# Gated linear attention and a two-layer block on one core: the fourth unit's output transposed by DMA instead of TensorE, in an order written out as tables

## The chip, the cores and the metric

The kernel runs on one core of a Trainium2 chip. The metric is device time in microseconds (us); lower is better. A "unit" below is a piece of 256 tokens of one batch element; the units are numbered 0 to 11, so the fourth unit is unit 3.

## What is computed

The reference is a recurrent linear attention with a decay per channel, followed by a dense block of two layers with a squared ReLU. The shapes are B = 4, H = 8, S = 768, D = 48, and the dense block has 3072 tokens, width 384 and hidden width 2048; everything comes in and goes out as float32.

```
state = zeros(B, H, D, D)
for t in range(S):
    state = alpha[:, :, t, :, None] * state + k[:, :, t] (outer) v[:, :, t]
    y[:, :, t] = q[:, :, t] @ state
x = y with the heads side by side, one row of 384 for each token
out = (relu(x @ w_in) ** 2) @ w_out
```

## The kernel before

**Units.** The sequence is cut into three stretches of 256 tokens, which gives 12 units (`G`). For each unit g the four inputs alpha, k, q, v are loaded (`lda`, `ldk`, `ldq`, `ldv`, line 568, 384 KB each) into one of four raw buffers. ScalarE takes logarithms and exponentials of the decays (`lm`, `ln`, `ei`, `ea`, `ec`, `es`), TensorE sums them along the tokens (`m1i`), VectorE multiplies them into the queries and keys (`bk`, `ekm`, `eqm0`, `eqm1`), and `vc` casts v to bf16. From unit 3 on, queries and keys are transposed by two DMAs (`tr0`, `tr1`, line 762). TensorE then forms the scores (`p0`, line 940, into the PSUM tiles psX and psZ), VectorE masks them (`mk0`, `mk1`, line 951), TensorE forms the attention output in psX and the next unit's state in psZ (`y`, lines 832, 843, 811), VectorE updates the state (`sa`, `sc`, `sd`), and ScalarE copies the output to the bf16 tile xbf (`xe`, line 971).

**Transpose of the output.** The dense block needs the output with channels on the partitions, in one of four buffers xt. In units 0 to 3 TensorE does this with six transposing products into psX (`xt`, line 986) and VectorE or ScalarE copies the result to xt (`xv`, line 998 or 1000; for unit 3 it is ScalarE, line 1000). In the units of `DMA_X`, 4 to 11, one DMA that SyncE issues transposes xbf into xt (`xt`, line 992, 196,608 bytes), with the same bytes in another order, and the first layer reads xt with a stride that undoes that.

**Dense block.** The first layer of a unit is eight operations `s1_g_u` of six matmuls each (line 1042), which alternate between two PSUM banks of psWH. Each is followed by a ReLU (`re`, line 1050 on ScalarE or 1052 on VectorE), and then a square (`sq`, lines 1060 and 1064). The second layer is, for each half j of the unit's tokens, four operations `s2_g_j_0` to `s2_g_j_3` of four matmuls each (line 1089). They all accumulate into one PSUM bank, psO, which ScalarE or VectorE copies out (`oe_g_j`, line 1097 or 1099) before the other half may start. SyncE stores the unit (`out`, line 1109).

**Order.** The body of the kernel adds operations with the data that they read and write, a cost and a priority. `schedule` runs a model of the engines and of the queues, gives each operation an engine and a place in that engine's order, and a dictionary `SHIFT` moves single priorities. `fill` puts products on a tile of zeros (line 1143) into TensorE's idle times before the first dense products. `place` then decides which operation waits for which semaphore. Each engine executes its own list strictly in order, and so does SyncE, which issues nearly all DMAs: an operation that waits holds all that are behind it on that engine. Some starts are tied by hand: `lda` of a unit waits for the landing of the unit's before `ldq`, and `ldq` waits for the landing of the DMA `tr0` of the unit before.

**The stretch around the change.** Before the change the engines' lists are these (the text under the prediction uses the names):

```
TensorE  y3 m1i5 s2_2_0_0 s2_2_0_1 xt3 s2_2_0_2 s2_2_0_3 p0_4 s1_3_0 s2_2_1_0 .. s2_2_1_3 s1_3_1 s1_3_2 y4
         s1_3_4 s1_3_3 m1i6 s1_3_6 ..
ScalarE  re2_6 xe3 ei5 ea5 ec5 xv3 es5 oe2_0 re3_0 oe2_1 lm6 re3_1 ln6 xe4 re3_4 re3_3 ei6 ..
VectorE  sa4 sq2_6 sc4 bk5 sd4 lb5 ekm5 eqm1_5 eqm0_5 mk0_4 mk1_4 re3_2 ..
SyncE    lda5 ldk5 tr0_4 tr1_4 ldq5 ldv5 out1_1 lda6 ldk6 tr0_5 tr1_5 out2_1 xt4 ldq6 ldv6 lda7 ..
```

Of the kernel before, what the change touches and what calls it, by code (L numbers as in the profile page):

```python
# [2 lines left out]

# [3 lines left out]
ALU = mybir.AluOpType  # L7
# [7 lines left out]
class Op:  # L15


    __slots__ = ("alts", "eng", "fn", "cost", "prio", "deps", "idx", "lag", "sem", "start", "end", "pos", "name",
                 "users", "ndeps", "mode", "ready", "land")

    def __init__(self, alts, prio, name):
        self.alts, self.prio, self.name = alts, prio, name
        self.eng = self.fn = self.cost = None
        self.deps = {}
        self.lag = 0
        self.sem = None
        self.users = []
        self.pos = None
        self.mode = ("F", "F")
        self.ready = 0.0  # L30
        self.start = self.end = self.land = None


class Program:

    HOP = 35
    PE_LATENCY = 170
    DMA_FIRST = {"sp": 1300, "act": 1300, "pool": 2000}  # L40
    PACKET = (("win", 172), ("wout", 490), ("ld", 22), ("tr", 18), ("xt", 18), ("out", 125))
    SBUF_ONLY = ("pr", "bk", "aq", "ekm", "eqm", "sq", "sb", "sd")
    BIAS = {"pool": 300}
    DMA_LAST = {"sp": 800, "act": 800, "pool": 1900}
    SWITCH = 95
    HALVED = {"qks": 3, "kqt": 3, "raw": 3, "ek": 3, "eq": 3, "acm": 2, "laf": 2}
    AFFINITY = 2500

    SHIFT = {
        "aq2": -248, "aq3": -1491, "bk2": 5224, "bk3": -2010, "bk5": 1601, "bk6": -3855, "ea0_0": 13157,  # L50
        "ea1": -1949, "ea1_0": 12558, "ea2": 2000, "ea3": -1980, "ea4": -1414, "ea5": -2487, "ea6": 81,
        "ec0_0": 20747, "ec1": -746, "ec1_0": 11544, "ec2": 2000, "ec3": -2160, "ec4": -1533, "ec5": 2471,
        "ei0_0": 10906, "ei1": -1289, "ei1_0": 11939, "ei2": 2000, "ei3": 8259, "ei4": -2378, "ei5": 98, "ei6": -386,
        "ekm0_0": 11970, "ekm1": -1066, "ekm1_0": 10619, "ekm2": 5424, "ekm3": -1183, "ekm4": 175, "ekm5": 937,
        "ekm6": 1068, "eqm0_0": 12087, "eqm0_3": -1862, "eqm0_4": 3228, "eqm0_5": 3013, "eqm0_6": -440, "eqm1": 2398,
        "eqm1_0": 12786, "eqm1_3": 1310, "eqm1_4": 270, "eqm1_5": -275, "eqm1_6": -211, "eqm2": 2240, "es2": 2000,
        "es3": -2890, "es5": -2113, "es6": -1558, "et00_0": -6783, "et01_0": 2965, "et0_1": 18, "et0_2": 4740,
        "et10_0": 1180, "et11_0": 849, "et1_1": -8121, "et1_2": 9290, "kv0": 1952, "kv1": -5798, "kv2": -10315,
        "lb4": -1797, "lb5": 195, "lb6": 67, "lm4": -1578, "lm5": -1529, "lm6": -1532, "ln0_0": 10550, "ln1": -409,
        "ln1_0": 17073, "ln2": 2000, "ln3": -2160, "ln4": 564, "ln5": 4370, "ln6": -283, "m10_0": 4838, "m11": -338,  # L60
        "m11_0": 9538, "m1i2": 2121, "m1i3": -533, "m1i5": 400, "m1i6": -1147, "m1s2": 2468, "m1s3": 3167,
        "mk0_0": -1001, "mk0_1": 9322, "mk0_2": 5670, "mk0_3": -10630, "mk0_4": 4794, "mk0_5": -4832, "mk1_0": -830,
        "mk1_1": 1380, "mk1_2": 4510, "mk1_3": -10630, "mk1_4": 7108, "mk1_5": -124, "oe0_0": -3484, "oe0_1": -14385,
        "oe1_0": -724, "oe1_1": 2594, "oe2_0": -260, "oe2_1": -627, "oe3_0": 11805, "oe3_1": 30, "oe4_0": -7260,
        "oe4_1": -7260, "oe5_0": 5260, "oe5_1": 5260, "out0_1": -8010, "out1_1": 6560, "out2_1": 2593, "out3_1": 30,
        "out4_1": -7260, "out5_1": 5260, "p0_0": -830, "p0_1": -2249, "p0_2": 4532, "p0_3": -11271, "p0_4": 2163,
        "p0_5": -6910, "p1_0": -830, "pr2": 376, "pr3": 563, "pr4": -2031, "pr5": 4470, "pr6": -3765, "pr7": -5581,
        "re0_0": -253, "re0_1": -2327, "re0_2": -1810, "re0_3": -2805, "re0_4": 7066, "re0_5": -3141, "re0_6": 1463,
        "re0_7": -2710, "re1_0": -2540, "re1_1": -1766, "re1_2": -2620, "re1_3": -2792, "re1_4": 4740, "re1_5": 99,
        "re1_6": -833, "re1_7": 2948, "re2_0": -151, "re2_1": -240, "re2_2": 24, "re2_3": -68, "re2_4": -519,  # L70
        "re2_5": -240, "re2_6": 5363, "re2_7": 3246, "re3_0": -3327, "re3_1": -1860, "re3_2": -1860, "re3_3": -2293,
        "re3_4": -1860, "re3_5": -5935, "re3_6": -6334, "re3_7": -1379, "re4_0": -5850, "re4_1": -2100,
        "re4_2": -6410, "re4_3": -2118, "re4_4": -5850, "re4_5": -5850, "re4_6": -5850, "re4_7": -5850,
        "re5_0": 2020, "re5_1": 2020, "re5_2": 2020, "re5_3": 2020, "re5_4": 2020, "re5_5": 2020, "re5_6": 2020,
        "re5_7": 2020, "s1_0_0": -2767, "s1_0_1": -1766, "s1_0_2": -1810, "s1_0_3": -1898, "s1_0_4": 202,
        "s1_0_5": -2691, "s1_0_6": -5306, "s1_0_7": 405, "s1_1_0": -2620, "s1_1_1": -5074, "s1_1_2": -364,
        "s1_1_3": 596, "s1_1_5": -6169, "s1_1_6": -383, "s1_1_7": -1034, "s1_2_0": -739, "s1_2_1": -687,
        "s1_2_2": -5198, "s1_2_3": -900, "s1_2_4": -1700, "s1_2_5": -240, "s1_2_6": -45, "s1_2_7": -688,
        "s1_3_0": -1860, "s1_3_1": -2146, "s1_3_2": -1582, "s1_3_3": -1860, "s1_3_4": -3211, "s1_3_5": -435,
        "s1_3_6": -1113, "s1_3_7": -1860, "s1_4_0": -10307, "s1_4_1": -5990, "s1_4_2": -5519, "s1_4_3": -6913,  # L80
        "s1_4_4": 2151, "s1_4_5": -6468, "s1_4_6": -5850, "s1_4_7": -5850, "s1_5_0": 2020, "s1_5_1": 2020,
        "s1_5_2": 2020, "s1_5_3": 2020, "s1_5_4": 2020, "s1_5_5": 2020, "s1_5_6": 2020, "s1_5_7": 2020,
        "s2_0_0_0": -7231, "s2_0_0_1": -6402, "s2_0_0_2": -9571, "s2_0_0_3": -4462, "s2_0_1_0": -7570,
        "s2_0_1_1": -6433, "s2_0_1_2": -7346, "s2_0_1_3": -13759, "s2_1_0_0": -1010, "s2_1_0_1": -1010,
        "s2_1_0_2": 6229, "s2_1_0_3": 4046, "s2_1_1_0": -1010, "s2_1_1_1": -4318, "s2_1_1_2": 7177, "s2_1_1_3": 9016,
        "s2_2_0_0": 4117, "s2_2_0_1": -1305, "s2_2_0_2": -260, "s2_2_0_3": -56, "s2_2_1_0": -6696, "s2_2_1_1": -5458,
        "s2_2_1_2": -259, "s2_2_1_3": -817, "s2_3_0_0": 690, "s2_3_0_1": 30, "s2_3_0_2": 3360, "s2_3_0_3": 3274,
        "s2_3_1_0": 30, "s2_3_1_1": 30, "s2_3_1_2": 30, "s2_3_1_3": 30, "s2_4_0_0": -7260, "s2_4_0_1": -7260,
        "s2_4_0_2": -7260, "s2_4_0_3": -7260, "s2_4_1_0": -7260, "s2_4_1_1": -7260, "s2_4_1_2": -7260,
        "s2_4_1_3": -7260, "s2_5_0_0": 5260, "s2_5_0_1": 5260, "s2_5_0_2": 5260, "s2_5_0_3": 5260, "s2_5_1_0": 5260,  # L90
        "s2_5_1_1": 5260, "s2_5_1_2": 5260, "s2_5_1_3": 5260, "sa0": 752, "sa1": -2890, "sa2": -10750, "sa3": 3302,
        "sa4": 2124, "sa5": -3013, "sc0": 873, "sc1": 490, "sc2": -9676, "sc3": 1435, "sc4": 2632, "sc5": -2325,
        "sd0": -4084, "sd1": 5380, "sd2": -10750, "sd3": 5505, "sd4": -5377, "sd5": -6091, "sq0_1": -2853,
        "sq0_3": -1810, "sq0_5": -3567, "sq0_6": -2710, "sq0_7": -7881, "sq1_1": 4005, "sq1_3": -2620, "sq1_5": 2964,
        "sq1_6": 101, "sq1_7": 3337, "sq2_1": 589, "sq2_3": -240, "sq2_5": -2358, "sq2_6": -240, "sq2_7": -2552,
        "sq3_1": -1736, "sq3_3": -1860, "sq3_5": -2116, "sq3_6": -1860, "sq3_7": 1961, "sq4_1": -2012,
        "sq4_3": -7277, "sq4_5": -5850, "sq4_6": -5850, "sq4_7": -5850, "sq5_1": 2020, "sq5_3": 2020, "sq5_5": 2020,
        "sq5_6": 2020, "sq5_7": 2020, "tr00_0": 1401, "tr01_0": 1210, "tr0_1": 1600, "tr0_2": 9290, "tr0_3": 329,
        "tr0_4": 730, "tr0_5": -1980, "tr0_6": -5474, "tr10_0": 505, "tr11_0": 3673, "tr1_1": 3514, "tr1_2": 14909,
        "tr1_3": 410, "tr1_4": 7738, "tr1_5": -1980, "vc0": 26092, "vc1": 2583, "vc2": 5594, "vc3": -2160,  # L100
        "vc4": 1938, "vc5": 859, "vc6": -1098, "xe0": 2520, "xe1": -5132, "xe2": 1303, "xe3": 9345, "xe4": 4442,
        "xe5": -2372, "xt0": -210, "xt1": -5759, "xt2": 697, "xt3": 5663, "xt4": 139, "xt5": 3570, "xv0": -3144,
        "xv1": -5170, "xv2": -2990, "xv3": 6300, "y0": -3305, "y1": -7643, "y2": -2990, "y3": 6489, "y4": 4090,
        "y5": -543,
    }

# [1068 lines left out]
```

## Time and profile before

| | |
|---|---|
| time, median of 3 runs | 174.98 us (174.0 to 175.28) |
| span of the profiled execution | 174.5 us |
| TensorE matmuls busy | 169.1 us, 97% of the span |
| VectorE, ScalarE, GpSimd busy | 121.3, 117.6, 18.8 us |
| share of the 16 DMA engines | 71.4% by SyncE's queue, 12.1% by GpSimd's |
| moved by DMA | 33.36 MB |

The profile states no time of its own for the profiled execution but its span, which lies from the first to the last instruction. The span is half a microsecond under the median of the runs and inside their spread. TensorE's matmuls overlap and their ends are modelled, so an operation's start to the start of the next one is the better measure of what it costs.

### The profile page before, as it was taken

How to read it: one execution, taken by the hardware profiler on the slowest of the kernel's cores; microseconds unless marked ns; L12 is line 12 of the kernel's file. 1: busy time of each engine (PE TensorE's matmuls, PEld its weight loads, DVE VectorE, ACT ScalarE, POOL GpSimd, SP SyncE). 2: the span in 40 equal slices, each digit the busy share in tenths (PEclk: the TensorE clock that was granted, in tenths of full speed). 3: DMA queues.
4: the chain of work that ended last, by engine and by line, in shares of the span. 5: the costliest groups of instructions: out<-in, count | busy, mean ns of one | idle time of the engine just before them, and what ended most of it. 6: DMA issues, size and time to landing. Idle time of an engine off the chain costs nothing.

```text
span 174.5 us, 5094 instructions
## 1 busy us (share of the span) xinstructions
PE 169.1 (97%) x2237; PEld 130.5 (75%) x2237; DVE 121.3 (70%) x197; ACT 117.6 (67%) x211; POOL 18.8 (11%) x28
## 2 busy tenths in 40 slices
PE   7989999999999999999999999999999999999994
PEld 2556898856886697777788886778788697688773
DVE  5497799797967869866778966868849726322230
ACT  3848698868869569768768757378668564566440
POOL 3159010022102120000100000000200000000000
DMA  5999999979998999798998897999899690040022
GB/s 139 324 297 190 274 303 216 230 208 280 274 229 125 274 235 188 200 222 151 278 212 211 228 196 180 275 201 251 201 214 208 115 196 4 0 135 4 10 80 90
DMA packets 74743, 33.36 MB, mean 191 GB/s; under 512 B 71649, under 2 KB 71905, under 8 KB 74721
## 3 DMA queue, kind: packets, MB, share of 16 engines
q1 hardware_dynamic: 73184, 28.32, 71.4%
q0 software_dynamic: 1536, 4.72, 12.1%
q8 instruction: 17, 0.28, 0.7%
q14 instruction: 6, 0.04, 0.1%
HBM read 25.17 MB, written 4.72 MB: 171 GB/s over the span
## 4 chain that ended last, share of the span: by engine, by line
PE 56%; DMA 26%; ACT 6%; DVE 4%; SPq 3%; POOL 2%; issue 1%
PE psO L1089 22%; PE psWH L1042 22%; DMA raw<-in_v_dram 9%; DMA wout<-in_moe_w_out_dram 8%; DMA raw<-in_alpha_dram 5%; DMA raw<-in_q_dram 5%; SPq L568 3%; PE psO L1143 2%; POOL raw L568 2%; ACT rr L1050 2%; PE psX L843 2%; PE psX L1012 2%; ACT vbf L742 1%; PE psZ L811 1%; PE psX L832 1%; PE psX L940 1%
## 5 line engine op out<-in xcount | busy, mean ns | idle before, releaser
L1042 PE MATMUL psWH<-xt,win 128*128 128x256 bf16 x576 | 73.9, 275 | 0.5 <-ACT rr L1050 0.2
L1042 PEld LDWEIGHTS psWH<-xt,win 128*128 128x128 bf16 x576 | 65.0, 145 | 6.2 <-DVE rr L1052 1.6
L1089 PE MATMUL psO<-wout,gt 128*128 128x384 bf16 x368 | 68.9, 326 | 0.0
L1050 ACT ACTIVATE rr<-psWH 128x512 bf16<-128x512 f32 x83 | 48.9, 596 | 21.5 <-PE psWH L1042 20.0
L1089 PEld LDWEIGHTS psO<-wout,gt 128*128 128x128 bf16 x368 | 34.8, 98 | 18.3 <-DVE gt L1060 0.2
L1060 DVE TENSOR_TENSOR gt<-rr 128x1024 bf16<-128x1024 bf16 (+1 forms) x47 | 28.4, 608 | 25.1 <-ACT rr L1050 24.5
L951 DVE TENSOR_TENSOR pm<-psX,caus 128x1024 bf16<-128x1024 f32 x12 | 14.6, 1220 | 2.4 <-PE psZ L940 2.1
L951 DVE TENSOR_TENSOR pm<-psZ,caus 128x1024 bf16<-128x1024 f32 x12 | 14.6, 1216 | 1.5 <-PE psZ L940 1.4
L1097 ACT ACTIVATE osb<-psO 128x384 f32<-128x384 f32 x19 | 9.3, 489 | 6.8 <-PE psO L1089 6.3
L971 ACT ACTIVATE xbf<-psX 128x768 bf16<-128x768 f32 x12 | 9.7, 806 | 5.0 <-PE psX L832 4.1
L746 DVE TENSOR_TENSOR qks<-raw,eq 128x384 bf16<-128x384 f32 x18 | 10.3, 605 | 3.0 <-DMA raw<-in_q_dram 3.0
L1143 PE MATMUL psO<-zero 128*128 128x512 bf16 (+1 forms) x37 | 10.5, 417 | 1.3 <-DVE zero L489 1.3
L741 POOL CAST vbf<-raw 128x768 bf16<-128x768 f32 x4 | 3.7, 930 | 71.5 <-DMA raw<-in_v_dram 71.5
L1064 ACT ACTIVATE gt<-rr 128x512 bf16<-128x512 bf16 (+1 forms) x13 | 10.8, 828 | 0.4
L751 DVE TENSOR_TENSOR qks<-raw,ek 128x768 bf16<-128x768 f32 x11 | 10.7, 969 | 0.4 <-ACT ek L663 0.3
L1052 DVE TENSOR_SCALAR rr<-psWH 128x512 bf16<-128x512 f32 x13 | 8.9, 687 | 2.0 <-PE psWH L1042 1.6
L742 ACT ACTIVATE vbf<-raw 128x768 bf16<-128x768 f32 x7 | 5.9, 845 | 3.5 <-DMA raw<-in_v_dram 3.5
L717 ACT ACTIVATE la<-raw 128x384 f32<-128x384 f32 x8 | 4.2, 523 | 5.3 <-DMA raw<-in_alpha_dram 5.2
L1143 PEld LDWEIGHTS psO<-zero 128*128 128x128 bf16 x37 | 3.5, 108 | 4.6 <-issue 1.9
L906 DVE TENSOR_TENSOR smd<-psZ,sbd 128x384 bf16<-128x384 f32 x8 | 4.4, 554 | 3.4 <-PE psX L832 3.4
L675 DVE TENSOR_TENSOR prd<-raw 128x384 f32<-128x384 f32 x7 | 4.0, 569 | 2.9 <-DMA raw<-in_alpha_dram 2.9
L678 ACT ACTIVATE lab<-prd 128x384 bf16<-128x384 f32 x10 | 5.2, 520 | 1.1 <-POOL prd L677 0.6
(115 smaller groups left out, 165.9 us busy)
## 6 DMA issues: line engine op xcount, KB each, us to landing
raw<-in_alpha_dram SPq DMA_DIRECT2D x11, 384.0 KB, 4.2
raw<-in_k_dram SPq DMA_DIRECT2D x11, 384.0 KB, 5.1
raw<-in_q_dram SPq DMA_DIRECT2D x11, 384.0 KB, 4.2
raw<-in_v_dram SPq DMA_DIRECT2D x11, 384.0 KB, 4.8
out_dram<-osb SPq DMA_DIRECT2D x11, 384.0 KB, 4.3
win<-in_moe_w_in_dram POOLq DMA_DIRECT2D x2, 768.0 KB, 9.9
wout<-in_moe_w_out_dram POOLq DMA_DIRECT2D x2, 768.0 KB, 15.2
raw<-in_alpha_dram POOLq DMA_DIRECT2D x1, 384.0 KB, 9.7
```

The lines of the kernel that those rows point to most:

```text
L746: add("dve", lambda e, j=j, dst=dst: e.tensor_tensor(dst, RAW[r][:, 2, :, j, :].rearrange("p (n x) d -> p n x d", x=2), EQ[la][:, j].rearr ...
L751: add("dve", lambda e, a=a, E=E: e.tensor_tensor(QKS[qs][:, a, :, :, 0:D], RAW[r][:, 1 + a].rearrange("p h j d -> p j h d"), E[la][:].rear ...
L951: add("dve", lambda e, hf=hf, psT=psT: e.tensor_tensor(PM[pm][:, hf].rearrange("p r n j t -> p (r n) (j t)"), psT[:, :, :].rearrange("p r ...
L971: add("act", lambda e: e.activation(XBF[x2][:], psX[:, :, 0:HD], AF.Copy), act_ns(2 * HD), p0 + 6100, reads=[("ps", "X", 0), ("ps", "X", 1 ...
L1042: ins = pe.matmul(psH[hb][:, i * T:(i + 1) * T], WIN[:, kk, hidden(fj)], mov, start=(kk == 0), stop=(kk == KT - 1))
L1050: add("act", lambda e, hb=hb, rr=rr: e.activation(rr, psH[hb], AF.Relu), act_ns(512), pu + 600, reads=[("ps", "H", hb)], writes=[("rr", rb ...
L1052: alts={"dve": (lambda e, hb=hb, rr=rr: e.tensor_scalar(rr, psH[hb], 0.0, None, ALU.max), dve_ns(512))})
L1060: add("dve", lambda e, dst=dst, sq=sq: e.tensor_tensor(dst, sq, sq, ALU.mult), 148 + k * 267, pu + 1200, reads=[("rr", rb, h) for h in ran ...
L1064: "act": (lambda e, dst=dst, sq=sq: e.activation(dst, sq, AF.Square), act_ns(k * 512))})
L1089: ins = pe.matmul(psS, GT[gt][:, fj, j, :], WOUT[:, fj, :], start=(fj * parts % FT == 0), stop=((fj + 1) * parts % FT == 0))
L1097: add("act", lambda e, j=j, psS=psS: e.activation(OSB[ob][:, j], psS, AF.Copy), act_ns(DM), ps_ + 700, reads=[keyS], writes=[("osb", ob, j ...
L1143: pr.fill(lambda n: lambda pe: pe.matmul(psO[:, 0:n], ZERO[:, 0:128], ZERO[:, 0:n], skip_group_check=True), ((512, 216, 420), (256, 109, 2 ...
```

## The change

The order is no longer computed. `schedule`, `fill` and `SHIFT` are gone, and a dictionary `TABLES` names for each engine its operations in order (fillers as +512 or +256); `arrange` reads it, and `sequence` gives `place` a global order that respects it. Read against the order that the kernel before computes, the tables differ in these places:

- unit 3 is added to `DMA_X`: on TensorE the six products of `xt3` are gone, on ScalarE the copy `xv3` is gone;
- on SyncE the DMA `xt3` stands new behind `ldv5` and ahead of `out1_1`;
- on TensorE `s1_3_0` stands behind `s2_2_1_3` instead of ahead of `s2_2_1_0`;
- all else, the fillers included, stands in the same order.

With `xt3` on SyncE the waits follow: `xt3` waits for `xe3`, `p0_4` waits for `xe3` instead of `xv3`, `s1_3_0` waits for the landing of the DMA `xt3`.

There is one more edit. Two operations that only read the same PSUM bank were ordered by a wait, also where both are on the same engine. `add` now notes such pairs in `shared` and `place` leaves the wait out when both are on one engine. That takes a wait of ScalarE for its own operation just before from 21 operations: `ea` behind `ei` in all units and `ec` behind `ea` in units 0 to 7 (unit 0 does them in two halves of the heads).

```diff
     HALVED = {"qks": 3, "kqt": 3, "raw": 3, "ek": 3, "eq": 3, "acm": 2, "laf": 2}
-    AFFINITY = 2500
-    SHIFT = {
...
             if k[0] == "ps":
                 for r in self.readers.get(k, ()):
-                    op.deps.setdefault(r, False)
+                    if r not in op.deps:
+                        op.deps[r] = False
+                        op.shared.add(r)
...
-    def schedule(self):
...
-    def fill(self, make, sizes, until, after, cold):
...
+    def arrange(self, tables, make, after):
+
+        named = {o.name: o for o in self.ops}
+        assert len(named) == len(self.ops)
+        self.order = {}
+        for e, text in tables.items():
+            self.order[e] = []
+            for x in text.split():
+                if x[0] == "+":
+                    o = Op({e: (make(int(x[1:])), 0)}, 0, "fill")
+                    o.idx = len(self.ops)
+                    o.deps = {after: True}
+                    self.ops.append(o)
                 else:
...
+                    o = named.pop(x)
+                o.eng = e
+                o.fn, o.cost = o.alts[e]
+                o.pos = len(self.order[e])
+                self.order[e].append(o)
...
-                if d.sem is None and d.eng == o.eng == "pe":
+                if d.sem is None and d.eng == o.eng and (o.eng == "pe" or not raw and d in o.shared):
                     continue
...
+TABLES = {
+    "act": """
...
+        re2_1 es4 oe1_0 re2_2 re2_3 re2_4 re2_5 sq2_5 lm5 re2_7 ln5 oe1_1 re2_6 xe3 ei5 ea5 ec5 es5 oe2_0 re3_0
+        oe2_1 lm6 re3_1 ln6 xe4 re3_4 re3_3 ei6 re3_6 re3_5 ea6 sq3_5 ec6 re3_7 sq3_7 es6 re4_0 re4_1 vc6 re4_2
...
+    "pe": """
...
+        s1_2_6 s1_2_7 s2_1_1_2 s2_1_1_3 y3 m1i5 s2_2_0_0 s2_2_0_1 s2_2_0_2 s2_2_0_3 p0_4 s2_2_1_0 s2_2_1_1
+        s2_2_1_2 s2_2_1_3 s1_3_0 s1_3_1 s1_3_2 y4 s1_3_4 s1_3_3 m1i6 s1_3_6 s1_3_5 s2_3_0_0 p0_5 s1_3_7 s2_3_0_1
...
+    "sp": """
+        lda0 ldk0 ldq0 ldv0 lda1 ldk1 ldq1 ldv1 lda3 ldk3 ldq3 ldv3 lda4 ldk4 ldq4 ldv4 out0_1 tr0_3 tr1_3 lda5
+        ldk5 tr0_4 tr1_4 ldq5 ldv5 xt3 out1_1 lda6 ldk6 tr0_5 tr1_5 out2_1 xt4 ldq6 ldv6 lda7 ldk7 tr0_6 tr1_6
...
-    DMA_X = (4, 5, 6, 7, 8, 9, 10, 11)
+    DMA_X = (3, 4, 5, 6, 7, 8, 9, 10, 11)
...
-    pr.schedule()
-    pr.fill(lambda n: lambda pe: pe.matmul(psO[:, 0:n], ZERO[:, 0:128], ZERO[:, 0:n], skip_group_check=True),
...
+    pr.arrange(TABLES, lambda n: lambda pe: pe.matmul(psO[:, 0:n], ZERO[:, 0:128], ZERO[:, 0:n], skip_group_check=True),
+               zero)
     pr.place()
     pr.emit()
```

## The prediction, made before the changed kernel had run

> **What bounds the kernel now.** I read the page first, then the busy time by stretches, then the waits of TensorE, the chain that ended last, and the timeline around unit 3's transpose.
>
> ```profile
> span 174.5 us, 5094 instructions
> PE 169.1 (97%) x2237; PEld 130.5 (75%) x2237; DVE 121.3 (70%) x197; ACT 117.6 (67%) x211; POOL 18.8 (11%) x28
> ```
>
> TensorE is nearly full. The next view cuts the span in two from unit 3's output (54 us) on; columns are the length, busy time by engine with instructions, granted clock, DMA share and GB/s.
>
> ```profile
> 54.00:117.00 63.00, 62.50 (x899) 48.69 (x889) 49.61 (x78) 44.79 (x84) 2.65 (x3) 1.00 0.99 214
> 117.00:169.40 52.40, 52.23 (x615) 41.89 (x615) 28.50 (x44) 32.65 (x56) 1.25 (x1) 1.00 0.55 121
> ```
>
> From 117 us TensorE idles 0.17 us in 52: what is late there stays late. From 54 to 117 us it idles only 0.50 us, but the DMA engines are full too (0.99), so two things run side by side, TensorE's work and the chain of loads. The chain of work says which ends last:
>
> ```profile
> 67.57 0.59 SPq L568
> 68.15 0.04 issue
> 68.20 5.09 DMA raw<-in_v_dram
> 73.29 0.02 issue
> 73.31 0.85 ACT vbf L742
> 74.17 0.05 issue
> 74.21 0.27 PE psX L832 x8
> ```
>
> The load of unit 6's v (ldv6) stands on SyncE behind the transpose xt4 and ldq6 (the first line); it lands at 73.29, vc6 casts it, and y5 starts on TensorE at 74.21, 0.05 us after vc6. TensorE sat idle 0.20 us before it. So **time that TensorE wins ahead of 74 us is given back at y5, unless the loads come earlier too; and a load that comes later moves y5.**
>
> Now the timeline around the change:
>
> ```profile
> 55.76 1.57 SPq L1109 DMA_DIRECT2D out_dram<-osb  x1
> 56.02 0.50 PE L986 MATMUL psX<-ident,xbf 128*128 128x128 bf16 x6
> 56.36 1.46 PE L1089 MATMUL psO<-wout,gt 128*128 128x384 bf16 x8
> 56.56 0.81 ACT L1000 ACTIVATE xt<-psX 128x768 bf16<-128x768 bf16 x1
> 57.36 0.52 ACT L721 ACTIVATE eq<-la 128x384 f32<-128x384 f32 x1
> 57.86 0.49 ACT L1097 ACTIVATE osb<-psO 128x384 f32<-128x384 f32 x1
> 58.33 0.87 PE L1042 MATMUL psWH<-xt,win 128*128 128x256 bf16 x6
> 58.76 0.37 SPq L568 DMA_DIRECT2D raw<-in_alpha_dram  x1
> 59.04 2.76 PE L1089 MATMUL psO<-wout,gt 128*128 128x384 bf16 x16
> ```
>
> In order: out1_1 on SyncE, xt3, s2_2_0_2 and _3, the copy xv3, es5, oe2_0 (which frees psO), s1_3_0, lda6, and the four s2_2_1.
>
> **TensorE, removed.** Eight second-layer matmuls stand ahead of xt3 (from 54.73) and eight behind it (from 56.36). Sixteen take 2.60 us from start to start (59.04 to 61.64, where s1_3_1 starts), eight 1.30; 56.36 - 54.73 - 1.30 leaves 0.33 us for xt3. Gain: **0.33**.
>
> **TensorE, moved.** p0_4 started at 57.75, now 57.42; its inputs are there (xe3 ended at 55.41, sc4 at 55.93). What follows it could start 0.58 us later (57.75 to 58.33), at 58.00. Before, that was s1_3_0, and it covered oe2_0. Now it is s2_2_1_0, which writes psO and must wait for oe2_0. Losing xv3 does not make oe2_0 earlier: es5 ahead of it waits for lb5 on VectorE, which ended at 57.33 after five VectorE operations without a gap, and es5 started at 57.36. So oe2_0 ends at 58.35 as before and s2_2_1_0 starts 0.05 later: 58.40, a **new wait of 0.40**. The four s2_2_1 take 2.60 and some 0.06 for the change of shape behind p0_4, so s1_3_0 starts at 61.06, s1_3_1 at 61.71. s1_3_2 uses s1_3_0's PSUM bank and waits for re3_0, which starts 0.85 after s1_3_0 (0.91 before, less the 0.06) and takes 0.60: 62.51, plus 0.05. Without it s1_3_2 would start at 62.36, so **0.20 more**; before, re3_0 had long been done. y4 starts 0.75 after s1_3_2, at 63.31 against 63.04. Sum on TensorE: -0.33 + 0.40 + 0.20 = **+0.27**.
>
> **The added DMA.** xe3 ends at 55.41 and SyncE is through ldv5 at 55.72, so xt3 is issued at once. The other eight of its kind:
>
> ```profile
> L992 SPq DMA_TRANSPOSE xt<-xbf x8: 1212/1345/1940, 66.1 to 152.6; - x8
> DMA to landing us min/median/max: 2.7/3.3/4.0
> ```
>
> Its landing must come before 61.06. The kindest bound is 55.76 + 2.7 = 58.5. But ldv5 lies ahead of it, issued at 55.08 and landed 4.7 later (59.8), and landings follow issue here (ldq5 58.7, ldv5 59.8, out1_1 60.8). For its own 197 KB I take the two paces below, 344 and 172 GB/s: 0.57 or 1.14 us, so 60.4 to 60.9. The unkind bound is the slowest transpose, tr0_5, 7.0 us: 62.8. I take 60.9, close to the xt rows and the queue: just in time, nothing added, but with only 0.15 us to spare.
>
> **SyncE behind it.** Behind xt3 wait out1_1, lda6, ldk6, tr0_5, tr1_5, out2_1, xt4, ldq6, ldv6. xt3 holds SyncE 1.21 to 1.94 us (median 1.35), then out1_1 1.57: done at 58.7, at worst 59.3. lda6 waits for ldq5's landing (58.7) anyhow; it started after 1.43 us of idle SyncE. The issue is hidden, or late by 0.55 at worst.
>
> **DMA engines.** Here are the two stretches behind ldv5's issue:
>
> ```profile
> 57.00:59.50 2.50, 2.50 (x47) 1.77 (x45) 1.93 (x4) 1.61 (x4) 0.00 (x0) 1.00 1.15 344
> 59.50:61.00 1.50, 1.50 (x12) 0.89 (x10) 1.50 (x3) 0.33 (x1) 0.82 (x1) 1.00 0.65 172
> ```
>
> From 59.5 to 61.0 half the pace is unused: (344 - 172) x 1.5 = 258 KB, more than xt3's 197 KB. But in this hole out1_1 ends and lda6 begins, and both now come behind xt3. The bounds for lda6's landing are 0 late (all in the hole) and 0.57 late (none in it). I take **0.4**, nearer the upper one, because xt3 and the pushed out1_1 together fill the hole before lda6 gets going.
>
> **What a late lda6 moves.** On ScalarE lm6 waited for it until 63.02; behind it stand re3_1, ln6, xe4 and re3_4, nearly back to back up to 65.82, and s1_3_6 started at 65.88 on that. 0.4 late there is 66.28, beyond TensorE's own 65.88 + 0.27. On SyncE ldk6, tr0_5, tr1_5, out2_1, xt4, ldq6, ldv6 follow one another from 59.17 to 68.84 with no gap over 0.1 us, so ldv6 lands 0.4 later and y5 starts at 74.6. If nothing were late, y5 would still start at 74.21: TensorE's +0.27 uses up the wait there.
>
> **ScalarE's own waits.** ea5 starts 0.03 us after ei5 ends, where neighbours overlap by 0.10; so each removed wait frees some 0.13, 21 of them 2.7 us of ScalarE, and xv3 0.8 more. ScalarE idles a third of the span. In the chain its operations of that kind show twice, at 6.6 us (behind it VectorE is busy with the keys until 7.12) and at 91.9 (behind it stands SyncE, which does not wait for them). I cost this at nothing; with that cover gone it is worth 2 x 0.13 = 0.26 of gain.
>
> **Sum.** 0 to +0.57 at y5, taken as +0.4, carried through to the end: span 174.5 + 0.4 = 174.9. The runs' median lies 0.5 above the span, so 174.98 + 0.4 = **175.4 us**. That is no change: about 1% (1.75 us) is what a measurement of this kernel can tell.
>
> **A rule against the change.** The Trainium skill, "VectorE: DVE Perf Modes", section "The three transpose paths", lists 1309 ns for a 128x128 bf16 block by DMA against 390 ns on TensorE. As an estimate from that page, six blocks one after another would take 7.9 us, xt3 would land at 63.6 and s1_3_0 would wait 2.6 us. The trace disagrees: eight transposes of this size landed 2.7 to 4.0 us after issue, and a transposing matmul takes 219 ns. It is rival 1's mechanism with another price: by the page's figure alone the time would be 174.98 + 0.27 + 2.6 = 177.8 us, which gets 0.02 of that rival's chance.
>
> **The rivals.** (1) *Slower: xt3 lands late.* The place is s1_3_0, the point of decision a landing after 61.06; each microsecond beyond is one on TensorE, and SyncE's chain is late with it. The price with tr0_5's 7.0 us: 62.8 - 61.06 = 1.75, plus the 0.27: +2.0, **177.0 us**. For it: no other xt is issued right behind two loads of 384 KB, and transposes behind loads took up to 7.0 us. Against: those were of 262 KB, and no xt exceeded 4.0. Chance 0.20.
> (2) *Nothing arrives.* The hole swallows xt3, y5's wait the rest: **175.0 us**. For it the 258 KB; against it, the order in the queue. Chance 0.18.
> (3) *The 0.33 us reach the end*, with 0.26 of ScalarE's: -0.6, **174.4 us**. For it: TensorE is 97% busy and six products are gone. Against: psO, and the wait for vc6 at y5. Chance 0.12. This is also what would come of it if psO were free in time.
> (4) *The tables do not act as named.* The lists show no other moved operation. Chance 0.02.
>
> **How the numbers follow.** The forecast has 0.48. Its own range is 174.6 to 175.9 (bounds 0 and +0.57, and the 0.3 by which medians of such runs wander). With the rivals: 173.9 to 177.1. Slower by over 1% needs 1.75 us: most of rival 1 (0.15), and some unseen sum of lateness (0.03): 0.18. Faster by over 1% would take more than xt3 (0.33), the idle 0.67 after 54 us and ScalarE's 0.26 together: 0.05 for what I overlook. The rest, 0.77, is the same.
>
> **What would show it.** Right: a gap of about 0.4 us on TensorE ahead of s2_2_1_0, released by oe2_0; a short one ahead of s1_3_2, released by re3_0; none ahead of s1_3_0; y4 at 63.3; lda6 landing near 63.4; y5 at 74.6; the last matmul about 0.4 us later. Wrong: s1_3_0 released by the DMA xt3 (rival 1), or y5 before 74.1 with ldv6 landing earlier (rival 3).

## The result and the profile after

The changed kernel takes 176.09 us, median of 21 runs (175.13 to 177.16), against 175.38 us in 21 runs of the kernel before (174.0 to 178.7). The ratio is **1.005, with a 95% interval of 1.0027 to 1.0072**: slower by 0.88 us (0.47 to 1.26, the ratio times 175.38); the medians alone differ by 0.71. That is under the 1% named in the prediction, yet not nothing. A ratio leaves out executions more than 1.5% above the fastest of their kernel; the medians given beside it do not.

The runs state span and time of each execution, and the time is always 1.7 to 1.8 us above the span (here 176.13 and 174.4). By that, the execution of before that the prediction read, with its span of 174.5, took about 176.2 us and was one of the longer ones; the half microsecond between its span and the median compares different executions. Below, the trace of the first experiment (the order of before, 174.83 us) stands beside it as the more typical one.

The page of the profile after, its first lines:

```profile
span 174.4 us, 5080 instructions
PE 168.7 (97%) x2231; PEld 129.8 (74%) x2231; DVE 121.2 (69%) x197; ACT 116.1 (67%) x210; POOL 19.3 (11%) x28
```

Six matmuls (2237 to 2231) and one ScalarE operation (211 to 210) are gone, as the diff says. The table by stretches of after (columns as in the prediction) shows what came instead:

```profile
54.00:117.00 63.00, 61.90 (x870) 47.85 (x863) 49.62 (x78) 43.32 (x82) 2.65 (x3) 1.00 1.02 216
57.00:58.50 1.50, 1.24 (x37) 0.85 (x37) 1.48 (x3) 0.88 (x2) 0.00 (x0) 1.00 1.62 317
58.50:60.00 1.50, 1.50 (x11) 0.91 (x10) 1.50 (x3) 0.00 (x0) 0.00 (x0) 1.00 0.96 29
60.00:61.00 1.00, 0.75 (x6) 0.24 (x4) 1.00 (x1) 0.00 (x0) 0.67 (x1) 1.00 1.02 356
```

From 54 to 117 us TensorE idles 1.10 us instead of 0.50, 0.26 of it between 57.0 and 58.5 and 0.25 between 60 and 61. The third line is the one to remember: for 1.5 us the DMA engines count as busy (0.96) and move **29 GB/s**, ahead of the landing of `xt3`. Of the stretches that the prediction read here, none moved less than 172. In half microseconds:

```profile
58.50:59.00 0.50, 0.50 (x5) 0.30 (x4) 0.50 (x2) 0.00 (x0) 0.00 (x0) 1.00 2.48 68
...
59.50:60.00 0.50, 0.50 (x5) 0.30 (x4) 0.50 (x2) 0.00 (x0) 0.00 (x0) 1.00 0.08 10
```

The view counts a packet's bytes and time in the stretch in which it starts. So a share of 2.48 means packets that take long, and then hardly one starts (0.08). I call this a **lull** below. The packet records of the trace say which packets these are: the transpose is 768 packets of 256 bytes with a median of 18 ns, and in the lull 20 of them take over 0.3 us, up to 1.76 us.

The timeline of after around the change, with the wait and its releaser in brackets:

```profile
55.21 2.24 SPq L881 DMA_TRANSPOSE xt<-xbf  x1
...
57.94 2.77 PE L978 MATMUL psO<-wout,gt 128*128 128x384 bf16 x16 [0.26 <-ACT osb L986]
...
58.12 0.43 SPq L457 DMA_DIRECT2D raw<-in_alpha_dram  x1
...
60.96 2.45 PE L931 MATMUL psWH<-xt,win 128*128 128x256 bf16 x18 [0.25 <-DMA xt<-xbf]
```

The four `s2_2_1` wait for `oe2_0` (57.41 to 57.88), as forecast, and then `s1_3_0` waits for the transpose, which was not. The brackets count from modelled ends; against undisturbed starts of the same products, by which this text counts, the two waits are 0.33 and 0.41.

And the chain from there to y5 in after:

```profile
72.83 1.31 PE psWH L931 x12
74.14 0.20 PE psX L721 x8
```

y5 (the last line) follows TensorE's own work. The load of unit 6's v, which ended the wait there before, is no longer in the chain.

The start of y3 varies from 53.0 to 55.4 us between executions, for reasons ahead of the change (e6 and e11 wait 1.3 to 1.4 us at `p0_3` for the transposes of unit 3's queries and keys). Positions are therefore given from **y3's start** in the table. "Landing" is when a transfer has arrived; the runs e1 and so on are described below.

| us after y3's start | before | e1 | after | e2 | e3 | e4 | e6 | e7 | e10 | e11 | e12 |
|---|---|---|---|---|---|---|---|---|---|---|---|
| landing of the new DMA | - | - | 7.81 | 7.41 | - | 7.68 | 7.01 | 6.74 | 7.16 | 6.74 | 7.44, 8.11 |
| issue of lda6 | 5.28 | 5.40 | 5.02 | 5.76 | 5.43 | 5.20 | 4.12 | 6.10 | 5.58 | 4.30 | 7.09 |
| landing of lda6 | 9.52 | 9.59 | 9.94 | 10.06 | 8.78 | 9.78 | 9.11 | 10.13 | 9.62 | 8.77 | 10.92 |
| y4 starts | 9.56 | 9.56 | 10.24 | 9.56 | 9.76 | 12.44 | 9.52 | 9.51 | 9.56 | 9.56 | 9.56 |
| s1_3_6 starts | 12.39 | 12.46 | 12.92 | 12.94 | 12.45 | 15.13 | 12.20 | 13.01 | 12.49 | 12.24 | 13.80 |
| y5 starts | 20.73 | 20.52 | 20.97 | 21.00 | 20.49 | 23.17 | 20.24 | 21.08 | 20.56 | 20.29 | 21.94 |

### The profile page after: what moved, and what is told of

The parts are those of the page before. It is cut to its first block, busy times and chain, and to the rows that moved or that the text cites. A ratio compares the mean times of both kernels' runs of the same rounds, so it can differ in the third digit from the quotient of the medians.

```text
span 174.4 us, 5080 instructions
## 1 busy us (share of the span) xinstructions
PE 168.7 (97%) x2231; PEld 129.8 (74%) x2231; DVE 121.2 (69%) x197; ACT 116.1 (67%) x210; POOL 19.3 (11%) x28
## 4 chain that ended last, share of the span: by engine, by line
PE 60%; DMA 25%; ACT 4%; SPq 4%; POOL 3%; DVE 1%; issue 1%
PE psWH L931 26%; PE psO L978 25%; DMA raw<-in_alpha_dram 8%; DMA wout<-in_moe_w_out_dram 8%; SPq L457 4%; DMA xt<-xbf 3%; DMA raw<-in_v_dram 3%; DMA raw<-in_q_dram 2%; POOL raw L457 2%; PE psX L732 2%; ACT rr L939 2%; PE psX L901 2%; PE psZ L700 1%; PE psX L721 1%; PE psX L829 1%; POOL prd L566 1%
## 5 line engine op out<-in xcount | busy, mean ns | idle before, releaser
L939 ACT ACTIVATE rr<-psWH 128x512 bf16<-128x512 f32 x83 | 49.4, 596 | 25.7 <-PE psWH L931 23.9
L635 DVE TENSOR_TENSOR qks<-raw,eq 128x384 bf16<-128x384 f32 x18 | 11.0, 641 | 1.2 <-DMA raw<-in_q_dram 1.2
L593 DVE TENSOR_TENSOR ek<-ek,raw 128x384 f32<-128x384 f32 x10 | 5.5, 553 | 0.7 <-ACT ek L584 0.7
```

What stands on the lines that cost most here:

```text
L635: add("dve", lambda e, j=j, dst=dst: e.tensor_tensor(dst, RAW[r][:, 2, :, j, :].rearrange("p (n x) d -> p n x d", x=2), EQ[la][:, j].rearr ...
L939: add("act", lambda e, hb=hb, rr=rr: e.activation(rr, psH[hb], AF.Relu), act_ns(512), pu + 600, reads=[("ps", "H", hb)], writes=[("rr", rb ...
```

## The experiments

Two accounts are set against each other. By the **TensorE account** the loss is the waits of `s2_2_1_0`, `s1_3_0` and `s1_3_2`, which the moved and the removed products brought. By the **queue account** it is the added transfer, whoever waits for it: it makes the loads behind it late. All edits are made to the changed kernel. Each ratio is to the kernel before on the same chip, with its 95% interval.

**e1: the waits alone.** The order of before, with the 21 waits of ScalarE left out.

```diff
-  y3 m1i5 s2_2_0_0 s2_2_0_1 s2_2_0_2 s2_2_0_3 p0_4 s2_2_1_0 .. s2_2_1_3 s1_3_0 s1_3_1
+  y3 m1i5 s2_2_0_0 s2_2_0_1 xt3 s2_2_0_2 s2_2_0_3 p0_4 s1_3_0 s2_2_1_0 .. s2_2_1_3 s1_3_1
-  ei5 ea5 ec5 es5 oe2_0        (ScalarE)
+  ei5 ea5 ec5 xv3 es5 oe2_0
-  ldq5 ldv5 xt3 out1_1 lda6    (SyncE)
+  ldq5 ldv5 out1_1 lda6
-    DMA_X = (3, 4, 5, 6, 7, 8, 9, 10, 11)
+    DMA_X = (4, 5, 6, 7, 8, 9, 10, 11)
```

> The order of the kernel before, xt3 on TensorE and xv3 on ScalarE, with only ScalarE's 21 waits for its own reads left out. Theory TensorE (the loss is made by waits of TensorE around unit 3's first layer): no difference to before, within 0.2 us. Rival ScalarE (the freed waits matter): 0.3 us faster, about 0.998, and the first y operations earlier by as much.

0.999 (0.9955 to 1.0025), 175.09 us. The waits that were left out are worth nothing that can be measured; the 0.3 us of the rival lie inside the interval, so they are not excluded. The stretch of e1 where after had 29 GB/s moves 340:

```profile
58.50:60.00 1.50, 1.50 (x13) 1.08 (x12) 1.25 (x3) 0.60 (x1) 0.00 (x0) 1.00 0.95 340
```

**e2 and e11: a twin.** e1 and one DMA transpose of the same tile into a tile that nobody reads. TensorE, ScalarE and VectorE do exactly what they do in e1, in the same order; e11 is the same kernel on another chip.

```diff
-  ldq5 ldv5 out1_1 lda6
+  ldq5 ldv5 xd3 out1_1 lda6
+    XD = sb("xd", [128, KT, 2, 128], BF16, 1)
+        if g == 3:
+            add("sp", lambda e: e.dma_start_transpose(twin, src), .., reads=[("xbf", x2)], writes=[("xd", 0)], name="xd3", ..)
```

> As the run with the waits alone, and a DMA transpose of unit 3's output is issued behind ldv5 on SyncE as in the change, into a tile that nobody reads; the first layer still uses TensorE's transpose, in the old order. Theory TensorE: at most 0.1 us slower than before. Rival loads (the added transfer delays SyncE and the loads behind it): 0.4 to 0.6 us slower, 1.0025 to 1.0035, with ldv6 landing that much later against the start of y4.

> The twin DMA once more, on the same chip as the two runs before it. All theories: 1.0035 as before, 0.6 us slower, the standstill at 58 to 60 us, s1_3_6 waiting 0.6 us.

e2: 1.0035 (1.0 to 1.0069), 175.89 us; e11: 1.0045 (1.0016 to 1.0074), 176.2 us. With nothing moved and nothing waiting for it, the transfer costs, within the intervals, what the whole change costs. The chain of waits in e1 and then in e2 (start, length, what) shows the way it goes:

```profile
54.44 4.29 DMA raw<-in_q_dram
...
58.74 4.19 DMA raw<-in_alpha_dram
...
65.27 0.50 ACT rr L939
...
65.81 1.53 PE psWH L931 x12
...
73.94 0.20 PE psX L721 x8
```

```profile
57.96 0.22 SPq L888
...
58.23 0.57 SPq L1003
...
58.84 4.30 DMA raw<-in_alpha_dram
...
65.48 0.50 ACT rr L944
...
66.02 1.53 PE psWH L936 x12
...
74.15 0.20 PE psX L722 x8
```

The steps are those of the prediction: `lda6`, ScalarE's work on it (the full chain also has 1.0 us of GpSimd on it), `re3_4`, `s1_3_6`, and TensorE without a wait to y5. In e2 `lda6` lands 0.47 later after y3, `s1_3_6` starts 0.48 later and y5 0.48 later. Most of that is there before `lda6` is issued. In e1 it follows the landing of `ldq5` (the first line); in e2 `xd3` held SyncE for 3.13 us, the store came behind it, and `lda6` was issued 0.28 after that landing (58.84 after 58.56). From issue to landing it took 4.30 against 4.19. The 1.1 us of e2 from 58.4 on:

```profile
58.40:59.50 1.10, 1.10 (x10) 0.77 (x9) 0.92 (x2) 0.60 (x1) 0.00 (x0) 1.00 1.14 54
```

The lull is there too, so it does not come from the waits on TensorE. The trace of e11 does not show the price at y5 (20.29): in that execution TensorE waited 1.35 us at `p0_3`, ahead of y3, the loads were early by comparison (`lda6` 8.77), and the expected wait at `s1_3_6` did not come. What the transfer cost in that execution the trace does not show.

**e3 and e5: the rest without the DMA.** No transpose of unit 3 on any engine, xt3's tile filled once with a constant (so unit 3's dense block computes on that); `s1_3_0` at its new place (e3) or at its old one (e5).

```diff
-  ldq5 ldv5 xt3 out1_1 lda6
+  ldq5 ldv5 out1_1 lda6
+    add("pool", lambda e: e.memset(XT[3][:].rearrange("p k j t -> p (k j t)"), 0.125), 800, 0, writes=[("xt", 3)], name="zxt")
+        if g == 3:
+            return
   e5 alone:
-  p0_4 s2_2_1_0 .. s2_2_1_3 s1_3_0 s1_3_1
+  p0_4 s1_3_0 s2_2_1_0 .. s2_2_1_3 s1_3_1
```

> Unit 3's transpose is left out altogether: neither TensorE nor a DMA does it, and unit 3's dense block reads a constant tile. s1_3_0 stands behind s2_2_1_3 as in the change. Theory TensorE: waits of 0.3 to 0.4 ahead of s2_2_1_0 and 0.2 ahead of s1_3_2 against 0.33 won, none ahead of s1_3_0; 0.1 to 0.3 us slower than before. Rival loads: no added transfer, so 0 to 0.3 us faster.

> Unit 3's transpose is left out altogether and unit 3's dense block reads a constant tile; s1_3_0 stands in its old place, so it covers oe2_0 as before. y4 comes 0.33 us earlier after y3 than in the order of before (9.23 instead of 9.56). Theory loads (y5 cannot start before unit 6's v has landed and been cast): y5 stays about 20.5 after y3, and the time within 0.2 us of before. Rival TensorE: y5 0.33 earlier and 0.3 us faster, 0.998.

e3: 1.0006 (0.9972 to 1.0041), 175.73 us. e5: 1.0015 (0.9982 to 1.0049), 175.36 us. In e3's trace the waits of 0.33 us at `s2_2_1_0` and 0.19 at `s1_3_2` stand as in after, y4 is 0.20 late, and y5 is on time (20.49). So the TensorE account's two foreseen waits do not reach y5 in this trace, and the time shows no loss, though its interval (-0.5 to 0.7 us) would hide 0.2 us. In e5's trace y4 is at 9.22 and y5 at 19.95, 0.57 earlier than in e1, where the first theory had expected y5 to stay; the gain does not show in the time.

**e4: `s1_3_0` at its old place, with the DMA.**

```diff
-  p0_4 s2_2_1_0 .. s2_2_1_3 s1_3_0 s1_3_1
+  p0_4 s1_3_0 s2_2_1_0 .. s2_2_1_3 s1_3_1
```

> As the change, but s1_3_0 stands in its old place ahead of s2_2_1_0 and must wait there for the DMA's landing near 60.9. Theory TensorE: it starts 2.6 us later than before (58.33 to 60.95) and the operations behind it too; waits further on swallow 0.3 to 1.0 of it, so 1.6 to 2.3 us slower, 1.009 to 1.013. Rival loads: the loads rule the pace and TensorE catches up, 0.4 to 0.8 us slower.

1.0161 (1.0097 to 1.0225), 179.4 us. The timeline of e4:

```profile
61.71 0.88 PE L931 MATMUL psWH<-xt,win 128*128 128x256 bf16 x6 [3.15 <-DMA xt<-xbf]
```

3.15 us of waiting, y5 2.65 later than in e1, 2.8 us in time by the ratio. A wait of this size on TensorE does reach the end, and the move of `s1_3_0` is what spares the change most of it.

**e6 and e7: TensorE's waits taken away.** In e6 `oe2_0` frees psO ahead of `es5`; in e7 the transpose is also issued ahead of `ldv5`.

```diff
-  ei5 ea5 ec5 es5 oe2_0 re3_0
+  ei5 ea5 ec5 oe2_0 es5 re3_0
   e7 also:
-  ldq5 ldv5 xt3 out1_1
+  ldq5 xt3 ldv5 out1_1
```

> As the change, with oe2_0 ahead of es5 on ScalarE. The wait of 0.33 ahead of s2_2_1_0 goes. Theory landing (s1_3_0 waits for the DMA xt3, which lands near 60.9 whatever TensorE does): the wait ahead of s1_3_0 grows from 0.41 to about 0.74, y4 stays 10.2 after y3, the time stays that of the change (1.005). Rival psO: y4 0.33 earlier and 0.3 us won.

> As the run before, and the DMA xt3 stands ahead of ldv5 on SyncE. Theory TensorE: xt3 lands about 1 us earlier, near 59.8, s1_3_0 waits for nothing and y4 comes 9.4 to 9.5 after y3; 0.5 us won against the change, level with before. Rival loads: lda6 still lands 10 us after y3 and s1_3_6 waits 0.6 us for what follows from it, as with the twin DMA, so 1.003 as there.

e6: 1.005 (1.0016 to 1.0084), 176.47 us. e7: 1.005 (1.001 to 1.009), 176.86 us. The wait at `s2_2_1_0` fell to 0.08 us, that at `s1_3_0` to nothing, y4 came 0.7 earlier than in after, and the time stayed. In e6 the wait expected at `s1_3_0` was not there, because TensorE had waited 1.31 us at `p0_3` and the landing was early against y3 (7.01); as in e11, neither path shows at y5 (20.24). In e7, `ldq5`, just ahead of the transpose, lands 0.70 later than in e1, `lda6`, which waits for it, at 10.13, and `s1_3_6` waits 0.82 us: the queue's path alone puts y5 at 21.08. Issued ahead of `ldv5`, and so behind `ldq5`, the transpose shows the same lull:

```profile
58.50:60.00 1.50, 1.49 (x13) 0.90 (x10) 0.17 (x1) 0.40 (x1) 0.00 (x0) 1.00 0.65 32
```

**e8: the store out of the way.** e2 with `out1_1` behind `tr1_5`.

```diff
-  xd3 out1_1 lda6 ldk6 tr0_5 tr1_5 out2_1
+  xd3 lda6 ldk6 tr0_5 tr1_5 out1_1 out2_1
```

> As the run with the twin DMA, but the store out1_1 stands behind tr1_5 on SyncE instead of ahead of lda6. Theory loads (the queue ahead of lda6 is what costs): lda6 lands 0.4 to 0.5 us earlier, 9.5 after y3, the wait of 0.63 ahead of s1_3_6 falls to the 0.15 of the order before, and the time to within 0.2 us of before. Rival (the transpose itself disturbs the loads wherever the store stands): no change to the twin run, 1.0035.

1.0037 (1.0 to 1.0074), 176.16 us. `lda6` lands at 8.64 and the wait at `s1_3_6` is gone, but the store is now ahead of `xt4` and `ldq6`: y5 waits 0.61 and `s1_4_7` 0.98 us. The lateness was passed on, or the store makes its own there: no run moves the store without the twin.

**e9, e10: is it the transpose, and its place?** e9 puts the twin behind the store; e10 keeps e2's place and replaces the transpose by a plain copy of the same bytes.

```diff
   e9:
-  ldq5 ldv5 xd3 out1_1 lda6
+  ldq5 ldv5 out1_1 xd3 lda6
   e10:
-            add("sp", lambda e: e.dma_start_transpose(twin, src), ..
+            add("sp", lambda e: e.dma_start(plain, src), ..
```

> As the twin DMA, but the transpose stands behind the store out1_1 and ahead of lda6 on SyncE instead of right behind the load ldv5. Theory standstill (a transpose that follows a load in the queue holds the DMA engines nearly still for over 1 us, one that follows a store does not, as xt4 does not): no stretch under 60 GB/s between 58 and 60.5 us, the added transfer fits the half-used stretch, lda6 lands within 0.2 us of its time without the twin (9.6 after y3), and the time is within 0.2 us of before. Rival bytes (197 KB more in the queue ahead of lda6 cost the same wherever they stand): lda6 0.4 us late and 1.0035.

> As the twin DMA in the change's place behind ldv5, but a plain copy of the same 197 KB from tile to tile instead of a transpose. Theory standstill: no stretch under 60 GB/s, the copy lies in the half-used stretch, lda6 within 0.2 us of 9.6 after y3, time within 0.2 us of before. Rival bytes: as the twin, lda6 at 10.06 after y3 and 1.0035.

e9: 0.9988 (0.995 to 1.0027), which is **inconclusive**: the median of all twelve executions is 176.36 us against 175.52 of the kernel before, a ratio of 1.0048. e10: 1.0022 (0.9988 to 1.0057), 175.73 us, between the two groups and apart from neither. The traces say more than the times. The slowest stretch of e9, then the stretch of e10 behind `ldv5`:

```profile
59.50:60.00 0.50, 0.50 (x5) 0.30 (x4) 0.50 (x1) 0.00 (x0) 0.50 (x1) 1.00 0.13 25
```

```profile
59.60:61.10 1.50, 1.50 (x13) 1.07 (x11) 1.07 (x3) 0.60 (x1) 0.00 (x0) 1.00 1.09 401
```

With a plain copy of 196,608 bytes in the queue the engines move 401 GB/s, and `lda6` is on time (9.62 against 9.59 in e1). The transpose behind the store still has a lull, but of 0.5 us; `lda6` lands at 9.30 and y5 starts at 20.39. That a lull comes behind loads alone, as the expectation had it, is therefore not borne out.

**e12: two twins.** A dose test: `xd3 xd4` in the place of `xd3`.

```diff
-  ldq5 ldv5 xd3 out1_1
+  ldq5 ldv5 xd3 xd4 out1_1
```

> Two twin DMAs, one behind the other, behind ldv5. Theory standstill: one standstill for both, then 0.6 to 0.9 us for the second's own bytes, and SyncE is past its 1.43 us of slack ahead of lda6 by 1.3 us; lda6 lands about 1 to 1.5 us later than with one twin, and the time is 1.0 to 1.5 us above it, 1.009 to 1.012. Rival (the loads have room): 1.0035 to 1.005 as with one.

1.0109 (1.0062 to 1.0156), 177.07 us. `lda6` lands 1.33 later than in e1, and TensorE waits twice on the way to y5. The slowest half microsecond of the engines there, SyncE's issue of `xd4`, and one of the two waits:

```profile
59.50:60.00 0.50, 0.50 (x6) 0.30 (x4) 0.50 (x2) 0.48 (x1) 0.00 (x0) 1.00 0.94 111
...
58.76 1.29 SPq L891
...
65.63 0.88 PE L939 MATMUL psWH<-xt,win 128*128 128x256 bf16 x6 [0.52 <-ACT rr L947]
```

y5 is 1.42 later than in e1. The second transpose costs no less than the first (0.64% on top of 0.45%, within the intervals). But the standstill that was expected is not there: 111 GB/s is the least of any half microsecond from 57.0 to 62.5 us. The twins held SyncE for 2.54 and 1.29 us, and `lda6` was issued 1.63 after the landing of `ldq5` that it waits for, then took 3.83 us. In this trace the price is SyncE's lateness and not a lull.

**Together.** The six kernels with one DMA transpose of unit 3 behind a load (after, e2, e6, e7, e8, e11; not e4 with its long wait) have a mean ratio of 1.0045 (1.0035 to 1.005), the three without it (e1, e3, e5) 1.0004 (0.999 to 1.0015), the one with two 1.0109. Most pairs of the first two groups are not clear of doubt, since their intervals overlap (e5 and e2); only after and e1 are just apart. The order of these ten, and the dose, is what shows that the transfer is the cost: 0.4% or 0.7 us. The ratio of e9, also a transpose, lies with those without one; by the medians of all executions it lies with the transposes (1.0048 among 1.0033 to 1.0079, against 0.9988 to 1.0024 without and 1.0012 for e10's copy). No kernel here is faster than the kernel before by more than the noise.

## Why the prediction was right or wrong

The forecast, 175.4 us and no change, has the right side of nothing and about half the size: +0.4 against +0.88 (0.47 to 1.26). Of the 0.69 us between 175.4 and 176.09, 0.40 is the base, three runs with a median of 174.98 where 21 have 175.38; 0.3 is the sum. The 176.09 lie 0.2 above the forecast's own range (174.6 to 175.9) and inside the one with the rivals (173.9 to 177.1).

**TensorE's terms, right.** Removed 0.33; the wait for psO 0.33 (forecast 0.40); the wait for `re3_0` 0.19 (0.20).

**`xt3` just in time, nothing added: wrong.** This is the step that failed. The landing at 60.91 is the forecast's 60.9 to the hundredth, but by luck: y3 started 0.38 earlier in this execution, and from y3 the landing is 7.81 instead of 7.42. `s1_3_0` waited 0.41 us. So rival 1's mechanism, which the prediction had named as its sign of being wrong, is there with a quarter of its price, and y4 is 0.68 late instead of 0.27. Working with absolute times of one execution hid how little 0.15 us of room is.

**`lda6` 0.4 late: right in size** (9.94 against 9.52, 0.42), **wrong in the reason.** The prediction let `xt3` flow at 172 to 344 GB/s into a half-used hole. It did not flow: 29 GB/s for 1.5 us, and `lda6` took 4.92 us from issue to landing where before's took 4.24. The row that says so was in the profile of before, five microseconds further on, ahead of the landings of `tr0_5` and `tr1_5` (66.78 and 67.47):

```profile
65.50:66.00 0.50, 0.48 (x8) 0.34 (x6) 0.47 (x2) 0.50 (x2) 0.00 (x0) 1.00 2.31 64
66.00:66.50 0.50, 0.50 (x6) 0.50 (x7) 0.50 (x2) 0.50 (x2) 0.00 (x0) 1.00 0.11 16
```

The prediction took the pace of stretches without a transpose in them for a transpose. And `ldv5` ahead of it, issued at 54.53, landed after 5.75 us instead of 4.7. The Trainium skill, "DMA: Bandwidth & Descriptors", section "Queues, rings and completion order", says that each DMA engine takes the descriptors of one issuing engine in ring order. The trace agrees as far as it goes: `ldv5`, `xt3`, `out1_1`, `lda6` land at 60.28, 60.91, 61.93 and 63.04, in the order of issue. That fits a hold on one being passed to all behind it, but does not show it.

**SyncE hidden: not quite.** `xt3` held it 2.24 us, beyond the forecast's 1.94, and `out1_1` 0.57. From y3 `lda6` was issued at 5.02 (5.28 before), but only because `ldq5` landed early too: against that landing it was 0.31 us late (58.12 after 57.81), and 0.02 in before. The 1.43 us of idle SyncE were used up. The forecast's worst case, 0.55, covers this; with two transposes (e12) it is 1.63, and the loads are late with it.

**y5 by `ldv6`, 0.4 later: half wrong.** y5 is 0.24 later than in before's trace and 0.45 later than in e1, near the forecast. `ldv6` is late as forecast against e1 (19.68 after y3 against 19.21), though not against before's trace (19.81), where it was late without the change. But y5 did not wait for it: it was set by TensorE in after, and by `lda6` through `s1_3_6` in e2 and e7. **Two paths of nearly the same length, 0.45 to 0.56 us, run side by side** in these traces, TensorE's waits and the late load; e3 takes away the late load and the wait for the landing, e7 TensorE's waits, and only without the transfer does the loss go. The sentence that time won ahead of 74 us is given back at y5 did not hold in e5's trace (19.95).

**ScalarE's waits at nothing: not contradicted** (e1). Rival 3's gain of 0.33 does not show in the time even where nothing stands against it (e5, 1.0015).

**What stays open.** y5 accounts for 0.45 of 0.88 us, and in the traces of e6 and e11 for none. Past y5 the two traces differ by waits for `lda10` (0.72 and 0.27 at `s1_7_3` and `s1_7_4` in after, 0.35 and 0.26 in before, none in e1), which also differ between executions without the DMA (0.38 and 0.26 in e3). From y5 to the last product the traces take 96.9 to 97.9 us without a transpose of unit 3 by DMA and 97.0 to 98.0 with it. Whether the transfer makes such waits more frequent, one trace for each kernel cannot tell. Nor was it found why some packets of a transpose take so long, why its issue holds SyncE for 1.27 us in e11 and 3.13 in e2, how much of the price is the lull and how much SyncE, or whether e9's place is really free.

## What to carry to other kernels

Where TensorE and the chain of loads are both full, as here, work taken from TensorE and given to the DMA queue can be paid for in the loads behind it, and neither side's waits alone show the price: cost the transfer by a twin that nobody reads. Count the issuing engine as well as the transfer: see how long it holds back the next load's issue. A hole in the DMA engines' pace is room only for a transfer that flows like its neighbours; look in the trace for the pace around a transfer of the same kind. Reckon positions from an event just ahead of the change, for executions of one kernel differ by more than the effect.

## What the runs showed of the hardware

Ahead of the landing of a DMA transpose of 196,608 bytes queued behind loads of 384 KB, the DMA engines moved 29 GB/s for 1.5 us (after), 54 for 1.1 us (e2) and 32 for 1.5 us (e7), where with a plain copy in the same place they moved 401 and in the order without it 340. The transpose is 768 packets of 256 bytes; 20 of them took over 0.3 us in after and in e2, up to 1.76 and 1.19 us, where the median is 18 ns. It is not always so: with two transposes in that place (e12) no half microsecond from 57.0 to 62.5 us moved less than 111. The issue of such a transpose held SyncE for 2.24 us (after), 3.13 (e2) and 1.27 (e11), that of the copy for 1.81 (e10). `xt4`, which follows `tr1_5` and a store, has no lull of its own: 236 GB/s from 67.5 to 69.0 us of after. The Trainium skill, "DMA: Bandwidth & Descriptors", section "Rules for kernel authors", has "A transpose next to ordinary DMAs needs nothing"; that speaks of the data, and in time the runs show a price of 0.4%.

Executions of one kernel lie as far apart as 174.0 and 176.6 us (18 of the 21 of before are within that), and y3 between 53.0 and 55.4 us after the start in the traces; y5, counted from y3, differs by 0.7 us between e2 and e11, which are one kernel. A difference of a few tenths between two traces carries nothing by itself.
